# Linear attention in a two-layer transformer stack: value projection reassociated to x^T k, and the output weights folded into one matrix

## Chip, cores, metric

The kernel runs on one core of a Trainium2 chip. The metric is the device time of one execution in microseconds (us), as the median of several runs. Engines: PE is the tensor engine (matmuls), PEld its weight loads, DVE the vector engine, ACT the scalar engine, POOL is GpSimd, SP issues the DMA. The granted clock is the share of its full clock that PE had, by the profile. PE's results land in PSUM, which these kernels use as eight banks; a bank is used again after DVE or ACT has read it out (an eviction).

## The reference, cut to what matters

Four layers in turn, A B A B, on x of 2048 tokens by 1024 features, bf16. A is linear attention with 32 heads of 32; B is a gated feed-forward layer (1024 to 3584 and back), which the change leaves alone.

```python
def A(x, wqkv, wo):                       # x is layer-normed
    q, k, v = split(x @ wqkv)             # 32 heads of 32
    pq, pk = phi(q), phi(k)               # phi(t) = t+1 if t>0 else exp(t), + 1e-6
    kv  = einsum("bhsd,bhse->bhde", pk, v)
    z   = einsum("bhsd->bhd", pk)
    num = einsum("bhqd,bhde->bhqe", pq, kv)
    den = einsum("bhqd,bhd->bhq", pq, z)[..., None] + 1e-6
    return (num / den) @ wo
```

## The kernel before

Tokens come in 16 tiles of 128, four tiles to a group. Each layer A has four projections (k, v, q, out): per projection 16 tiles x 2 halves x 8 matmuls of 128x512. Between them stand the narrow matmuls of the heads, with 132 columns, 128 for four heads' k^T v and four of ones that give z; the same shape again turns q into numerators and denominators.

```python
def kv_unit(t):                           # after k and v of tile t
    for c in range(KD):                   # 8 matmuls, 132 columns each
        nc.tensor.matmul(out=acc[0][:, c, 0:ZW], lhsT=pk[t % 4][:, c * P:(c + 1) * P],
                         rhs=vz[t % 4][:, c, :], ...)
def o_unit(t):                            # numerators and denominators of tile t
    for c in range(KD):                   # 8 matmuls, 132 columns each
        nc.tensor.matmul(out=ps[:, c, 0:ZW], lhsT=pqT[g % 3][:, c, tl * P:(tl + 1) * P],
                         rhs=KVz[:, c, :], start=True, stop=True)
    ...                                   # reciprocal, then one 128x1024 multiply on DVE
def phi(ps, dst):                         # per 128x512 block
    nc.scalar.activation(out=e, in_=ps[:], func=ACT.Exp)
    nc.vector.tensor_scalar(out=e, in0=e, scalar1=1.0, scalar2=1e-6, op0=ALU.min, op1=ALU.add)
    nc.vector.scalar_tensor_tensor(out=dst, in0=ps[:], scalar=1.0 + 1e-6, in1=e, ...)
...
# first layer: per tile two k blocks AND two v blocks, so PE spends 7.4 us on a tile
for t in range(g * TPG, (g + 1) * TPG):
    units += [k_unit(t, 0), k_unit(t, 1)]
    ...
    units += [v_unit(t, 0), v_unit(t, 1)]
```

Normalising a tile takes statistics on DVE, a reciprocal root in small steps on POOL, an apply on DVE, and a transpose: on PE for tiles 0 to 3 of the first layer, by DMA otherwise.

Of the kernel before, what the change touches and what calls it, by code (L numbers as in the profile page):

```python
# [25 lines left out]
def kernel(  # L26
# [23 lines left out]
    MM = 4  # L50
    HC = P // 32
    ZW = P + HC
    ZS = NB // 2
# [13 lines left out]
    KVz = const.tile([P, KD, ZW], BF16, tag="KVz", name="KVz")  # L67

    hT = H[:].rearrange("p (f s) -> p f s", s=G)
    pk = [H[:, i * D:(i + 1) * D] for i in range(4)]  # L70
    o0 = 4 * D
    vz = [H[:, o0 + i * KD * ZW:o0 + (i + 1) * KD * ZW].rearrange("p (c f) -> p c f", f=ZW) for i in range(4)]
    o0 += 4 * KD * ZW
    onat = [H[:, o0 + i * D:o0 + (i + 1) * D] for i in range(4)]
    o0 += 4 * D
    eb = [H[:, o0 + i * NB:o0 + (i + 1) * NB] for i in range(3)]
    oT = [H[:, i * KD * G:(i + 1) * KD * G].rearrange("p (c s) -> p c s", s=G) for i in range(2)]
    wk = Wr[0:2]
    wv = Wr[2:4]
    wo = [Dr[i][:].rearrange("p (k n) -> p k n", n=NB) for i in (0, 1)]  # L80
    pqT = [Dr[i][:].rearrange("p (c s) -> p c s", s=G) for i in (2, 3, 4)]
    wq = [Dr[i][:].rearrange("p (k n) -> p k n", n=NB) for i in (5, 6)]
    wd = [Dr[f // 4][:, (f % 4) * D:(f % 4 + 1) * D] for f in range(KF)]
    ring = [Wr[0], Wr[1], Wr[2], Wr[3], xT[2], xT[3]]

# [12 lines left out]
    def load_k(n):  # L98
        load(wk[n][:], wqkv_v[:, :, D + n * NB:D + (n + 1) * NB])

    def load_v(n):
        load(wv[n][:], wqkv_v[:, :, 2 * D + n * NB:2 * D + (n + 1) * NB])

    def load_q():
        for n in range(2):
            load(wq[n], wqkv_v[:, :, n * NB:(n + 1) * NB])
# [17 lines left out]
    load_x(0)  # L124
    for k in range(0, KD, 2):
        load(wk[0][:, k:k + 2, :], wqkv_v[:, k:k + 2, D:D + NB])
        if k == 0:
            load_x(1)
    load_x(2)
    load_x(3)  # L130
    load_k(1)
    load_v(0)
    load_v(1)
    for t in range(TPG, 2 * TPG):
        load_x(t)
# [6 lines left out]
    mask = const.tile([P, ZW], F32, tag="mask", name="mask")  # L142

    def make_mask():
        nc.gpsimd.memset(mask[:], 0.0)
        for b in range(HC):
            nc.gpsimd.memset(mask[32 * b:32 * b + 32, 32 * b:32 * b + 32], 1.0)
            nc.gpsimd.memset(mask[32 * b:32 * b + 32, P + b:P + b + 1], 1.0)

# [4 lines left out]
    zps = psum.tile([P, NB], F32, tag="mm", bufs=MM, name="zps")  # L154
# [6 lines left out]
    def ln_stats(t):  # L161
        st = small.tile([P, 2, 6], F32, tag="st", name="st")
        for c in range(2):
            nc.vector.bn_stats(out=st[:, c, :], in_=X[:, t, c * NB:(c + 1) * NB])  # L164
        mv = small.tile([P, 2], F32, tag="mv", bufs=2 * TPG, name="mv")
        nc.vector.bn_aggr(out=mv[:], in_=st[:])
        ve = small.tile([P, 1], F32, tag="ve", name="ve")
        nc.gpsimd.tensor_scalar(out=ve[:], in0=mv[:, 1:2], scalar1=1e-5, scalar2=None, op0=ALU.add)
        rstd = small.tile([P, 1], F32, tag="rstd", bufs=2 * TPG, name="rstd")
        nc.gpsimd.tensor_tensor(out=rstd[:], in0=ve[:], in1=mhalf[:], op=ALU.pow)  # L170
        stat[t] = (mv, rstd)

    xns = {}

    def ln_apply(t):
        mv, rstd = stat.pop(t)
        xn = work.tile([P, D], BF16, tag="xn", name="xn")
        nc.vector.tensor_scalar(out=xn[:], in0=X[:, t, :], scalar1=mv[:, 0:1], scalar2=rstd[:],  # L178
                                op0=ALU.subtract, op1=ALU.mult)
        xns[t] = xn  # L180

    def transpose_tile(src, dst):
        nc.sync.dma_start_transpose(out=dst, in_=src)

    def tx(t, slot):

        def run():
            if t not in xns:
                ln_apply(t)
            tl = t % TPG  # L190
            transpose_tile(xns.pop(t)[:], xT[slot][:, :, tl * P:(tl + 1) * P])
        return run

    def tx_pe(t):

        def run():
            if t not in xns:
                ln_apply(t)
            src = xns.pop(t)
            pt = psum.tile([P, KD, P], BF16, tag="mm", bufs=MM, name="pt")  # L200
            for k in range(KD):
                nc.tensor.transpose(out=pt[:, k, :], in_=src[:, k * P:(k + 1) * P], identity=ident[:])
            nc.scalar.copy(out=xT[t // TPG][:, :, t % TPG * P:(t % TPG + 1) * P], in_=pt[:])
        return run

    def mm_tile():
        return psum.tile([P, NB], F32, tag="mm", bufs=MM, name="ps")

    def kv_tile():
        return psum.tile([P, KD, ZS], F32, tag="kv", bufs=1, name="kv")  # L210

    phis = [0]

    def phi(ps, dst):

        e = eb[phis[0] % 3]
        phis[0] += 1
        nc.scalar.activation(out=e, in_=ps[:], func=ACT.Exp)  # L218
        nc.vector.tensor_scalar(out=e, in0=e, scalar1=1.0, scalar2=1e-6, op0=ALU.min, op1=ALU.add)  # L219
        nc.vector.scalar_tensor_tensor(out=dst, in0=ps[:], scalar=1.0 + 1e-6, in1=e, op0=ALU.add, op1=ALU.max)  # L220


    def k_unit(t, n):
        def run():
            ps = mm_tile()
            xt, tl = xT[t // TPG], t % TPG
            for k in range(KD):
                nc.tensor.matmul(out=ps[:], lhsT=xt[:, k, tl * P:(tl + 1) * P], rhs=wk[n][:, k, :],  # L228
                                 start=(k == 0), stop=(k == KD - 1))
            phi(ps, pk[t % 4][:, n * NB:(n + 1) * NB])  # L230
        return run

    def v_unit(t, n):
        def run():
            ps = mm_tile()
            xt, tl = xT[t // TPG], t % TPG
            for k in range(KD):
                nc.tensor.matmul(out=ps[:], lhsT=xt[:, k, tl * P:(tl + 1) * P], rhs=wv[n][:, k, :],  # L238
                                 start=(k == 0), stop=(k == KD - 1))
            c = n * (NB // P)  # L240
            nc.scalar.copy(out=vz[t % 4][:, c:c + NB // P, 0:P], in_=ps[:].rearrange("p (c f) -> p c f", f=P))
        return run

    acc = []

    def kv_unit(t):

        def run():
            if t == 0:
                acc[:] = [kv_tile()]  # L250
            for c in range(KD):
                nc.tensor.matmul(out=acc[0][:, c, 0:ZW], lhsT=pk[t % 4][:, c * P:(c + 1) * P],  # L252
                                 rhs=vz[t % 4][:, c, :], start=(t == 0 and c % 2 == 0),
                                 stop=(t == NT - 1), skip_group_check=True)
            if t == NT - 1:
                nc.vector.tensor_tensor(out=KVz[:], in0=acc[0][:, :, 0:ZW],  # L256
                                        in1=mask[:].unsqueeze(1).to_broadcast([P, KD, ZW]), op=ALU.mult)
        return run

    def q_unit(g, c):  # L260
        def run():
            ps = mm_tile()
            n, cl = c // (NB // P), c % (NB // P)
            for k in range(KD):
                nc.tensor.matmul(out=ps[:], lhsT=wq[n][:, k, cl * P:(cl + 1) * P], rhs=xT[g][:, k, :],  # L265
                                 start=(k == 0), stop=(k == KD - 1))
            phi(ps, pqT[g % 3][:, c, :])
        return run

    def o_unit(t):  # L270

        def run():
            g, tl = t // TPG, t % TPG
            ps = kv_tile()
            for c in range(KD):
                nc.tensor.matmul(out=ps[:, c, 0:ZW], lhsT=pqT[g % 3][:, c, tl * P:(tl + 1) * P],  # L276
                                 rhs=KVz[:, c, :], start=True, stop=True)
            den = small.tile([P, KD, HC], F32, tag="den", name="den")
            nc.vector.tensor_scalar(out=den[:], in0=ps[:, :, P:ZW], scalar1=1e-6, scalar2=None, op0=ALU.add)
            nc.vector.reciprocal(out=den[:], in_=den[:])  # L280
            nc.vector.tensor_tensor(
                out=onat[tl].rearrange("p (c h e) -> p c h e", c=KD, h=HC),
                in0=ps[:, :, 0:P].rearrange("p c (h e) -> p c h e", h=HC),
                in1=den[:].unsqueeze(3).to_broadcast([P, KD, HC, 32]), op=ALU.mult)
        return run

    def to_unit(t):
        def run():
            tl = t % TPG
            transpose_tile(onat[tl], oT[(t // TPG) % 2][:, :, tl * P:(tl + 1) * P])  # L290
        return run
# [5 lines left out]
    def out_unit(t, n):  # L297
        def run():
            ps = mm_tile()
            tl = t % TPG  # L300
            for c in range(KD):
                nc.tensor.matmul(out=ps[:], lhsT=oT[(t // TPG) % 2][:, c, tl * P:(tl + 1) * P], rhs=wo[n][:, c, :],  # L302
# [37 lines left out]
    def stats_unit(t):  # L340
        return lambda: ln_stats(t)

# [178 lines left out]
```

## Time and profile before

| | before |
|---|---|
| time, median of 3 | 1650.54 us (1650.45 to 1650.82) |
| PE busy | 1632.5 of 1648.8 us |
| DVE, ACT busy | 537.9, 250.6 us |
| first layer A (0 to first gate matmul) | 248.64 us |
| first layer B | 580.16 us |
| second layer A | 236.88 us |

From the page of the kernel before: the span, the busy time of each engine with its instructions, and the chain of work that ended last by engine.

```profile
span 1648.8 us, 18785 instructions
...
PE 1632.5 (99%) x7882; PEld 762.9 (46%) x8040; DVE 537.9 (33%) x965; ACT 250.6 (15%) x422; POOL 53.8 (3%) x152
...
PE 98%; DVE 1%; issue 1%; DMA 0%; SPq 0%; POOL 0%; ACT 0%
```

PE is always busy, and the chain is PE from end to end. Every matmul has one weight load, so "PEld x8040" counts the matmuls (a few matmul records are missing, 7882).

The chain in order of time (start, duration, what) gives the cost of one matmul of each size:

```profile
36.11 0.47 PE kv L252 x8
36.58 1.73 PE ps L238 x8
```

Eight matmuls of 132 columns take 0.47 us, eight of 512 take 1.73 us: 59 and 216 ns each. The waits view of PE (who waited for whom, total, times, longest) has three lines:

```profile
PE pt L202 <- DVE xn L178: 2.7, 3, 1.5
PE kv L276 <- DVE KVz L256: 1.4, 2, 0.7
PE zps L156 <- DVE xT_73 L153: 1.2, 1, 1.2
```

### The profile page before, as it was taken

The page shows a single profiled execution, that of the slowest core. Times are in us where ns is not written, and L with a number is a line of the kernel's source. Part 1 is how long each engine was busy: PE and PEld are TensorE (multiplying, and loading weights), DVE is VectorE, ACT ScalarE, POOL GpSimd, SP SyncE. Part 2 cuts the span into 40 slices and gives each one's busy share as a digit, 9 for nine tenths or more (in the row PEclk, how much of TensorE's full clock was granted, in tenths as well). Part 3 has the DMA queues.
Part 4 walks back from the last instruction along what each step waited for, and adds up shares of the span by engine and source line. Part 5 has one row for each costly group of instructions (what it writes and reads, how often), then busy time and mean ns, then how long its engine had stood idle before and what let it go on. Part 6 is the DMA issues. An engine that isn't in the chain of part 4 may idle for free.

```text
span 1648.8 us, 18785 instructions
## 1 busy us (share of the span) xinstructions
PE 1632.5 (99%) x7882; PEld 762.9 (46%) x8040; DVE 537.9 (33%) x965; ACT 250.6 (15%) x422; POOL 53.8 (3%) x152
## 2 busy tenths in 40 slices
PE   9999999999999999999999999999999999999999
PEld 4444544444444444444444445444444444444444
DVE  5553873212211311222443348632132113211211
ACT  3333101100110110011023331011001101100110
POOL 2000000000000000000100000000000000000000
PEclk9999999999999999999999999999999999999999
DMA  6513459431640443063340044594225405422400
GB/s 189 169 26 101 66 115 306 153 103 41 173 155 15 127 154 102 28 177 102 77 128 1 1 115 73 144 306 150 72 68 172 157 23 165 150 81 64 153 4 23
DMA packets 244996, 182.63 MB, mean 111 GB/s; under 512 B 100528, under 2 KB 235696, under 8 KB 244912
## 3 DMA queue, kind: packets, MB, share of 16 engines
q1 hardware_dynamic: 244912, 181.43, 38.5%
q8 instruction: 63, 1.03, 0.3%
q14 instruction: 21, 0.17, 0.0%
HBM read 153.09 MB, written 4.19 MB: 95 GB/s over the span
## 4 chain that ended last, share of the span: by engine, by line
PE 98%; DVE 1%; issue 1%; DMA 0%; SPq 0%; POOL 0%; ACT 0%
PE ps L316 47%; PE ps L333 23%; PE ps L238 7%; PE ps L302 7%; PE ps L265 6%; PE ps L228 6%; PE kv L276 1%; PE kv L252 1%; DMA X<-in_A_x_dram 0%; SPq L96 0%; DVE st L164 0%; DVE KVz L256 0%; DVE D_82 L220 0%; ACT H L218 0%; DVE xn L178 0%
## 5 line engine op out<-in xcount | busy, mean ns | idle before, releaser
L320 DVE TENSOR_TENSOR H<-gs,ps 128x512 bf16<-128x512 f32 x224 | 154.1, 688 | 567.6 <-PE ps L316 530.8
L319 ACT COPY gs<-ps 128x512 f32<-128x512 f32 x224 | 131.3, 586 | 1047.8 <-PE ps L316 1024.9
L333 PEld LDWEIGHTS <-H 128*128 128x128 bf16 x1848 | 178.5, 98 | 208.7
L335 DVE TENSOR_TENSOR X<-X,ps 128x512 bf16<-128x512 bf16 (+1 forms) x66 | 44.2, 670 | 327.0 <-PE ps L333 296.5
L218 ACT ACTIVATE H<-ps 128x512 bf16<-128x512 f32 x128 | 76.4, 597 | 201.8 <-PE ps L228 92.9
L316 PEld LDWEIGHTS <-W_75 128*128 128x128 bf16 x640 | 62.6, 98 | 75.5
L316 PEld LDWEIGHTS <-W_74 128*128 128x128 bf16 x640 | 62.6, 98 | 75.5
L219 DVE TENSOR_SCALAR H<-H 128x512 bf16<-128x512 bf16 x128 | 37.3, 291 | 162.8 <-ACT H L218 162.8
L316 PEld LDWEIGHTS <-xT_73 128*128 128x128 bf16 x576 | 56.4, 98 | 68.0
L316 PEld LDWEIGHTS <-xT_72 128*128 128x128 bf16 x576 | 56.4, 98 | 68.0
L316 PEld LDWEIGHTS <-W_76 128*128 128x128 bf16 x576 | 56.4, 98 | 68.0
L316 PEld LDWEIGHTS <-W_77 128*128 128x128 bf16 x576 | 56.4, 98 | 68.0
L164 DVE BATCH_NORM_STATS2 st<-X 128x6 f32<-128x512 bf16 x128 | 80.8, 673 | 5.4 <-DMA X<-in_A_x_dram 5.4
L316 PE MATMUL ps<-xT_71,W_76 128*128 128x512 bf16 x316 | 75.4, 379 | 0.2
L316 PE MATMUL ps<-xT_70,xT_72 128*128 128x512 bf16 x312 | 75.2, 379 | 0.4
L316 PE MATMUL ps<-xT_70,xT_73 128*128 128x512 bf16 x314 | 75.3, 379 | 0.3
L316 PE MATMUL ps<-xT_71,W_77 128*128 128x512 bf16 x314 | 75.3, 379 | 0.3
L302 PEld LDWEIGHTS <-H 128*128 128x128 bf16 x512 | 49.3, 98 | 56.2
L316 PE MATMUL ps<-xT_71,W_74 128*128 128x512 bf16 x314 | 74.6, 379 | 0.4
L316 PE MATMUL ps<-xT_70,W_74 128*128 128x512 bf16 x314 | 74.6, 379 | 0.3
L316 PE MATMUL ps<-xT_70,W_75 128*128 128x512 bf16 x312 | 74.2, 379 | 0.3
L316 PE MATMUL ps<-xT_71,W_75 128*128 128x512 bf16 x314 | 74.3, 379 | 0.2
(88 smaller groups left out, 1742.9 us busy)
## 6 DMA issues: line engine op xcount, KB each, us to landing
W_74<-in_B_w_gate_dram SPq DMA_DIRECT2D x20, 1024.0 KB, 5.4
W_75<-in_B_w_up_dram SPq DMA_DIRECT2D x20, 1024.0 KB, 7.3
W_76<-in_B_w_gate_dram SPq DMA_DIRECT2D x18, 1024.0 KB, 5.4
W_77<-in_B_w_up_dram SPq DMA_DIRECT2D x18, 1024.0 KB, 7.3
xT_72<-in_B_w_gate_dram SPq DMA_DIRECT2D x18, 1024.0 KB, 5.3
xT_73<-in_B_w_up_dram SPq DMA_DIRECT2D x18, 1024.0 KB, 7.0
X<-in_A_x_dram SPq DMA_DIRECT2D x16, 256.0 KB, 7.8
out_dram<-X SPq DMA_DIRECT2D x31, 128.0 KB, 1.7
```

The costliest lines, as they stand in the source:

```text
L164: nc.vector.bn_stats(out=st[:, c, :], in_=X[:, t, c * NB:(c + 1) * NB])
L218: nc.scalar.activation(out=e, in_=ps[:], func=ACT.Exp)
L219: nc.vector.tensor_scalar(out=e, in0=e, scalar1=1.0, scalar2=1e-6, op0=ALU.min, op1=ALU.add)
L228: nc.tensor.matmul(out=ps[:], lhsT=xt[:, k, tl * P:(tl + 1) * P], rhs=wk[n][:, k, :], start=(k == 0), stop=(k == KD - 1))
L238: nc.tensor.matmul(out=ps[:], lhsT=xt[:, k, tl * P:(tl + 1) * P], rhs=wv[n][:, k, :], start=(k == 0), stop=(k == KD - 1))
L265: nc.tensor.matmul(out=ps[:], lhsT=wq[n][:, k, cl * P:(cl + 1) * P], rhs=xT[g][:, k, :], start=(k == 0), stop=(k == KD - 1))
L302: nc.tensor.matmul(out=ps[:], lhsT=oT[(t // TPG) % 2][:, c, tl * P:(tl + 1) * P], rhs=wo[n][:, c, :], start=(c == 0), stop=(c == KD - 1))
L316: nc.tensor.matmul(out=ps[:], lhsT=w[:, k, j * P:(j + 1) * P], rhs=xT[g % 2][:, k, :], start=(k == 0), stop=(k == KD - 1))
L319: nc.scalar.copy(out=gs[:], in_=gp[:])
L320: nc.vector.tensor_tensor(out=hT[:, f, :], in0=gs[:], in1=up[:], op=ALU.mult)
L333: nc.tensor.matmul(out=ps[:, 0:hi - lo], lhsT=hT[:, f, tl * P:(tl + 1) * P], rhs=wd[f][:, cols], start=(f == 0), stop=(f == KF - 1))
L335: nc.vector.tensor_tensor(out=X[:, t, cols], in0=X[:, t, cols], in1=ps[:, 0:hi - lo], op=ALU.add)
```

## The change

The intent is to take PE work away. k^T v per head needs v = x w_v. It is rewritten as (x^T k) turned by w_v: x^T k is accumulated once over all 16 tiles at full width, then multiplied by w_v per head, masked, and multiplied by the output weights to one 1024x1024 matrix KVo. So the narrow matmuls per tile go. q is divided by the denominators before its transpose, token-major, on DVE; the sums of k for the denominators are running sums on DVE. All x^T k needs all tiles of k, so in the first layer the k stage of 16 tiles stands alone at the start, with no v blocks between. To feed it, part of the normalisation moves to ACT. The eight PSUM banks become one pool.

```diff
+    def xk_unit(j, n):                    # x^T k, 16 matmuls of 512 columns
+            for t in range(NT):
+                nc.tensor.matmul(out=ps[:], lhsT=xn_a[t][:, j * P:(j + 1) * P], rhs=pk[t][:, n * NB:(n + 1) * NB], ...)
+    def over_den(t):                      # the division, token-major
+        nc.vector.tensor_tensor(out=prod, in0=pq[:], in1=zb, op=ALU.mult)
+        nc.vector.tensor_reduce(out=den[:], in_=prod.rearrange("p (h e) -> p h e", e=32), ...)
+        nc.vector.tensor_scalar(out=den[:], in0=den[:], scalar1=1e-6, ...)
+        nc.vector.reciprocal(out=den[:], in_=den[:])
+        nc.vector.tensor_tensor(out=pq[:]..., in0=pq[:]..., in1=den[:]..., op=ALU.mult)
+        tx(pq[:], t, t // TPG)
+    def kvo_unit(c, n):
+        nc.tensor.matmul(out=ps[:], lhsT=KVT[0][:, c, :], rhs=wo[n][:, c, :], start=True, stop=True)
+        if c % 4 == 3:
+            nc.vector.tensor_copy(out=KVo[n][:, c, :], in_=ps[:])
+        else:
+            nc.scalar.copy(out=KVo[n][:, c, :], in_=ps[:])
+    def ln_stats_act(t, xn):              # statistics of one tile in four on ACT
+        nc.scalar.activation(out=xn, in_=X[:, t, :], func=ACT.Identity, accum_out=add[:, 0:1])
+        nc.gpsimd.tensor_scalar(out=mv[:, 1:2], in0=add[:, 0:1], scalar1=-1.0 / D, ...)
+        nc.scalar.activation(out=xn, in_=X[:, t, :], func=ACT.Square, bias=mv[:, 1:2], accum_out=add[:, 1:2])
+        ...                               # variance and reciprocal root on POOL
+    def ln_apply_act(t, xn):              # apply on ACT; its offset on POOL
+        nc.gpsimd.tensor_scalar(out=off[:], in0=mv[:, 0:1], scalar1=rstd[:], scalar2=-1.0, ...)
+        nc.scalar.activation(out=xn, in_=X[:, t, :], func=ACT.Identity, scale=rstd[:], bias=off[:])
 ... first layer, groups 1 to 3 (t is the first tile of the group, u the k blocks of the group before):
+                ln_stats(t)
+                ln_stats_act(t + 1, xn_a[t + 1])
+                u[0]()
+                norm(t)                   # ln_apply_act, then the DMA transpose
+                ln_stats(t + 2)
+                u[1]()
+                norm(t + 1)
 ... then 16 x^T k units, the first 7 (second layer: 4) in a row, the rest between the first 11 q tiles, then
+        kv_unit()
+        do(q[24:28])
+        for i in range(4):
+            kvo_units(i)()
+            q[28 + i]()
```

(Removed lines and buffer changes are left out.)

## The prediction

> **What bounds the kernel now.** TensorE. The page shows PE busy 1632.5 us of 1648.8 (99%), full granted clock in all 40 slices, and the chain that ended last is 98% PE. The waits view of PE lists only 5.3 us. A 128x512 matmul costs 216 ns start to start (eight in 1.73 us in the chain); a 128x132 one of lines 252 and 276 about 59 ns (eight in 0.47 us). DVE is busy 33%, ACT 15%. So time follows the sum of matmul columns, plus about 15 us of ends and start-up stalls.
>
> **What changes on PE.** By the built programs, both layers A together: 512 matmuls of 132 columns go (-30.0 us). Four projections' worth stay: k, q, x^T k in place of v, out. Added are 128 narrow 128x128 (+7.2 us at 56 ns, the spacing of the transposes) and 40 of 512 columns (+8.6 us). Net -14 us, 0.9%, all on the critical path. Layers B, over 70% of the span, stay.
>
> **What changes elsewhere.** The q stage gets heavy on DVE. Per token tile: two phi at 0.98 us (291+692 ns), as before; then the division: product, reduction and scaling over 1024 columns, each estimated at 1.22 us (the trace's 128x1024 fp32 operation takes 1224 ns; the Trainium skill, "VectorE: DVE Perf Modes", perf-mode tier table, gives tensor_reduce and fp32 tensor_tensor only the 1x rate, so no discount), plus 0.18 and 0.35 us. Together 6.2 us per tile. PE has 3.45 us per tile plus interleaved x^T k units: 6.3 us in the first layer, 7.2 in the second, so DVE keeps up for tiles 0 to 10. Tiles 11 to 15 have no such filling: DVE about 5 x 6.2 + 4 = 35 us against 24 of PE. Eight PSUM buffers taken in turn, four KVo evictions queued on DVE behind divisions, let PE run ahead only 4 to 9 us. I estimate 2 to 6 us of stall per layer A, say 4.
>
> Fifteen running sums (1.22 us each) hide behind x^T k units. In the first layer k uses a tile every 3.45 us instead of k and v every 7.4, so normalisation must be faster: DVE 13 us per group of four against 13.8 of PE, helped by ACT (11 us). I give it 0 to 4 us of stalls, say 0.5. Start-up gains about 1 us (first k no longer waits for the second transpose), and the waits for masked KV (1.4 us) go.
>
> **Sum.** 1650.5 - 14 - 2.5 + 8 (q tails) + 0.5 = 1642, 8 in 10 within 1633 to 1652. Within 2%: 0.95; faster 0.02, slower 0.03.
>
> **What would show it.** Right: PE's matmul count and columns fall by 14 us' worth; the waits view of PE shows new waits on DVE (phi, the KVo copy) of 4 to 12 us, at the end of each q stage, DVE over 90% busy there; layers B keep their length to 0.5 us. Each wide division operation takes 1.1 to 1.3 us. The sums stage shows no wait over 2 us.
>
> **What would make it wrong.** Division operations slower than 1.22 us (then tiles 0 to 10 become DVE-bound, up to +1 us per tile per layer for each extra us); DMA transposes of q stuck behind the 4 MB weight loads; layer B starting late, since a gate/up load now waits for the last out unit; no stall at all because the PSUM slack suffices (1632 to 1635).

## More of the kernel before

The timeline of PE shows where the layers begin; the first number is the start in us.

```profile
25.59 1.67 PE L238 MATMUL ps<-W_76,xT_70 128*128 128x512 bf16 x7
...
248.64 1.67 PE L316 MATMUL ps<-xT_70,W_74 128*128 128x512 bf16 x7
...
828.80 1.46 PE L228 MATMUL ps<-W_74,xT_70 128*128 128x512 bf16 x6
...
1065.68 1.67 PE L316 MATMUL ps<-xT_70,W_74 128*128 128x512 bf16 x7
```

The first of these is the first v block: by 25.59 us the eight k blocks of the first group are done. The other three are the start of the first layer B, of the second layer A and of the second layer B; their differences are the stage lengths in the table.

## The result, and the profile after

| | before | changed |
|---|---|---|
| time, median of 4 | 1650.68 us | 1648.53 us (1647.9 to 1649.08) |
| ratio of fast runs | | 0.9986, 95% interval 0.9969 to 1.0004 |
| first layer A | 248.64 us | 251.95 us |
| first layer B | 580.16 us | 580.16 us |
| second layer A | 236.88 us | 231.00 us |

Ratios here are the mean time of one kernel's fast runs over that of the other's fast runs of the same rounds, so they are not quite the ratio of the medians quoted. (The kernel before was timed again here, hence 1650.68.) The forecast was a gain of 8.5 us; the gain was 2.1 us, not told apart from none by its interval. The stage lengths come from single profiles, where they repeat closely: the second layer A took 231.00 or 231.01 us in every run that did not touch it. The start of the program is less steady: the first k block began between 8.35 and 9.09 us in runs whose program is the same up to there, and 9.09 is the profile of the changed kernel itself.

The page of the changed kernel, the same lines as before:

```profile
span 1646.2 us, 18145 instructions
...
PE 1622.5 (99%) x7547; PEld 744.7 (45%) x7696; DVE 646.2 (39%) x1050; ACT 266.8 (16%) x444; POOL 58.0 (4%) x159
...
PE 94%; DVE 3%; issue 1%; ACT 1%; POOL 0%; DMA 0%; ACTq 0%; DVEq 0%
```

The matmuls fell from 8040 to 7696, as counted from the programs. But PE's share of the chain fell from 98% to 94%: DVE, ACT and waits between them now stand on it. The timeline of PE, stage starts:

```profile
251.95 1.24 PE L351 MATMUL ps<-xT_70,W_74 128*128 128x512 bf16 x5
...
832.11 1.24 PE L233 MATMUL ps<-W_74,xT_70 128*128 128x512 bf16 x5
...
1063.11 1.24 PE L351 MATMUL ps<-xT_70,W_74 128*128 128x512 bf16 x5
```

The second layer A became 5.88 us shorter, the first 3.31 us longer; -5.88 + 3.31 is the whole difference of the two spans, 2.6 us. So the question is what the first layer lost. The waits view of PE:

```profile
PE ps L233 <- DMA xT_71<-W_77: 3.9, 1, 3.9
PE ps L233 <- ACT xT_70 L215: 2.2, 2, 1.1
PE ps L233 <- DMA xT_73<-D_84: 2.2, 1, 2.2
PE zps L153 <- DVE xT_73 L150: 1.2, 1, 1.2
PE ps L233 <- DVE pq L225: 1.1, 2, 0.5
PE ps L319 <- DVE D_80 L321: 1.1, 2, 0.5
PE pt L214 <- DVE W_76 L194: 0.6, 1, 0.6
PE ps L233 <- ACT D_81 L323: 0.6, 2, 0.3
```

The two waits for a transposing DMA (3.9 and 2.2 us) are the first tile of group 1 and of group 3 in the first layer's k stage. Waits on DVE and ACT at lines 233 and 319 with two occurrences each are the ends of the two q stages, 1.4 us per layer. The timeline of PE around the first wait:

```profile
24.85 1.89 PE L233 MATMUL ps<-W_75,xT_70 128*128 128x512 bf16 x7
30.68 3.55 PE L233 MATMUL ps<-W_74,xT_71 128*128 128x512 bf16 x8 [3.94 <-DMA xT_71<-W_77]
34.07 1.89 PE L233 MATMUL ps<-W_75,xT_71 128*128 128x512 bf16 x8
```

The last block of group 0 ends at 26.58 (24.85 + 1.73), 1.0 us later than the same eight blocks before the change. Then PE stands for 4.1 us, and the next eight matmuls take 3.39 us instead of 1.73. The stretches view of the changed kernel says why (columns: busy us and instructions of PE, PEld, DVE, ACT, POOL; granted clock; DMA share; GB/s):

```profile
30.60:34.10 3.50, 3.42 (x9) 1.23 (x10) 1.40 (x4) 2.74 (x5) 1.32 (x4) 0.51 0.39 75
```

The granted clock is 0.51. The Trainium skill, "TensorE: Matmul & The Clock Gate", "What's actually happening", states that PE falls back to half clock after an idle window of about 3.4 us and needs a busy one to return. This wait of 4.1 us and the 3.39 us after it agree (the last section has gaps that do not); here the fall costs 1.66 us on top of the wait.

The ledger of the first layer, from these views: late by 1.0 us at the end of group 0, wait 4.1, half clock 1.7, wait for tile 12 2.4 (a matmul's record is 0.16 us longer than its spacing, 379 against 216 ns, so the waits view shows each wait 0.16 us short). That is 9.2 us where the prediction had a net gain of 0.5 (0.5 of stalls less 1 of start). The first term is the least certain: this profile has the latest start of all, by up to 0.7 us.

The chain that led to the first wait, from the timeline of the other engines:

```profile
22.84 0.57 POOL L169 TENSOR_TENSOR rstd<-ve,mhalf 128x1 f32<-128x1 f32 x1
23.49 0.25 POOL L182 TENSOR_SCALAR mv<-add 128x1 f32<-128x1 f32 x1
...
23.77 1.15 ACT L183 ACTIVATE W_77<-X,mv 128x1024 bf16<-128x1024 bf16 x1 [1.85 <-POOL mv L182]
...
24.92 0.58 ACT L223 ACTIVATE e<-ps 128x512 bf16<-128x512 f32 x1
...
25.53 0.29 DVE L224 TENSOR_SCALAR e<-e 128x512 bf16<-128x512 bf16 x1 [3.09 <-ACT e L223]
...
25.93 0.27 POOL L201 TENSOR_SCALAR off<-mv,rstd 128x1 f32<-128x1 f32 x1
26.23 1.24 ACT L203 ACTIVATE W_77<-X,off,rstd 128x1024 bf16<-128x1024 bf16 x1 [0.73 <-POOL off L201]
```

Tile 4's reciprocal root is ready at 23.41 us, but its offset, a tiny operation, runs on POOL only at 25.93: in program order the variance and root of tile 5, which wait for its second moment on ACT, stand in front of it. The Trainium skill, "Perfetto Trace Analysis", "Tensor Engine Instruction (MATMUL, LD_WEIGHTS)", calls the queues of ACT, DVE and GPSIMD strictly first in, first out; these lines agree. Meanwhile ACT had waited 1.85 us for POOL, whose turn had come late because tile 4's statistics stood ahead there; and DVE waited 3.09 us for ACT's exp. No engine is full, all wait for each other. From the end of the apply at 27.47 to PE's next matmul at 30.68 another 3.2 us go to the transpose by DMA, so the 2.5 us of queueing are most of the 4.1 us wait and not all of it.

### The profile page after: what moved, and what is told of

Its sections match the earlier page's. It is cut to its first block, busy times and chain, and to the rows that moved or that the text cites. A ratio compares the mean times of both kernels' runs of the same rounds, so it can differ in the third digit from the quotient of the medians.

```text
span 1646.2 us, 18145 instructions
## 1 busy us (share of the span) xinstructions
PE 1622.5 (99%) x7547; PEld 744.7 (45%) x7696; DVE 646.2 (39%) x1050; ACT 266.8 (16%) x444; POOL 58.0 (4%) x159
## 4 chain that ended last, share of the span: by engine, by line
PE 94%; DVE 3%; issue 1%; ACT 1%; POOL 0%; DMA 0%; ACTq 0%; DVEq 0%
PE ps L351 47%; PE ps L368 23%; PE ps L233 10%; PE ps L337 7%; PE ps L245 7%; DVE st L161 1%; DVE H L225 1%; ACT e L223 0%; PE zps L153 0%; DVE pq L225 0%; DVE e L224 0%; DVE D_82 L289 0%; DVE den L291 0%; POOL rstd L169 0%; ACT D_81 L323 0%
## 5 line engine op out<-in xcount | busy, mean ns | idle before, releaser
L368 PEld LDWEIGHTS <-H 128*128 128x128 bf16 x1848 | 178.6, 98 | 208.7
L223 ACT ACTIVATE e<-ps 128x512 bf16<-128x512 f32 x128 | 75.8, 595 | 174.7 <-PE ps L233 163.4
L161 DVE BATCH_NORM_STATS2 st<-X 128x6 f32<-128x512 bf16 x122 | 77.4, 675 | 2.3 <-DMA X<-in_A_x_dram 2.3
L368 PE MATMUL ps<-D_81,H 128*128 128x512 bf16 (+2 forms) x264 | 66.0, 373 | 0.4
L368 PE MATMUL ps<-D_78,H 128*128 128x512 bf16 (+2 forms) x262 | 65.9, 372 | 0.3
```

Of the source, the lines that this page charges most:

```text
L161: nc.vector.bn_stats(out=stat[t][0][:, c, :], in_=X[:, t, c * NB:(c + 1) * NB])
L223: nc.scalar.activation(out=e[:], in_=ps[:], func=ACT.Exp)
L368: nc.tensor.matmul(out=ps[:, 0:hi - lo], lhsT=hT[:, f, tl * P:(tl + 1) * P], rhs=wd[f][:, cols], start=(f == 0), stop=(f == KF - 1))
```

## The experiments

Theory A: the first layer's k stage ate the gain, by waits on normalisation. Rivals: B, the waits only show a limit of DVE and ACT in that stage; C, the division at the end of the q stages costs more than it shows. Changes are against the changed kernel unless said otherwise. It was timed once, before the experiments; only the kernel before was timed in the same rounds as each of them. Differences between medians of about 1 us therefore say little, and the stage lengths decide: the k stage (last column) took 67.05 to 67.10 us in all five profiles in which nothing of it was touched.

| run | time, us | first layer A | second layer A | first k to first x^T k |
|---|---|---|---|---|
| changed | 1648.53 | 251.95 | 231.00 | 67.10 |
| k reads group 0 (wrong result) | 1646.52 | 250.37 | 231.00 | 66.03 |
| order only | 1647.05 | 251.38 | 231.00 | 66.60 |
| no tail division (wrong result) | 1643.14 | 249.17 | 228.91 | 67.07 |
| filler matmuls | 1648.27 | 251.57 | 231.01 | 67.26 |
| banks in turn (1 run, unknown) | 1657.76 | 257.24 | 235.48 | 68.78 |
| new start | 1641.87 | 245.84 | 231.01 | 60.59 |
| product on GpSimd | 1656.06 | 255.12 | 234.95 | 67.06 |
| combined | 1641.51 | 248.31 | 228.91 | 60.84 |
| KVo on ACT (1 run, unknown) | 1643.15 | 249.21 | 228.90 | 67.07 |
| KVo on ACT, timed | 1643.64 | 249.56 | 228.90 | 67.05 |
| even pace | 1634.74 | 241.09 | 228.90 | 57.98 |

The kernel before, beside these, had medians of 1650.43 to 1650.64 us. The last column is the k stage of the first layer; its 256 matmuls need 55.3 us at 216 ns.

### k reads group 0

```diff
-        xt, tl = xT[t // TPG], t % TPG
+        xt, tl = xT[0], t % TPG          # k of the first layer only; wrong result on purpose
```

> Wrong result on purpose: in the first layer the k units of groups 1 to 3 read the transposed tiles of group 0, so that they wait for no normalisation; nothing else changes. Theory A (the first layer's k stage ate the gain: PE stood 3.9 us for tile 4 and 2.2 us for tile 12, and ran 1.7 us long at half clock after the first wait): the two waits and the slow matmuls go, the time falls by 7.8 us, from 1648.5 to about 1640.7. Rival B (those waits hide a limit of DVE and ACT throughput in that stage): the waits move to PSUM buffers and the gain is under 3 us. Rival C (the loss is the division at the end of the q stages): under 1 us.

The time fell by 2.0 us, not 7.8, and the profile has 0.5 us of it as an earlier start and 1.1 us in the k stage. The waits on the DMA were gone, but the waits view of PE in this run begins with a line that was not there:

```profile
PE ps L233 <- DVE H L225: 6.0, 7, 1.3
```

PE ran ahead until the PSUM banks were full and then waited for DVE's phi. So theory A in its simple form fell, and rival B was nearer: whatever PE is spared at one place, the stage makes it wait at another. In this run DVE was busy 36.7 and ACT 35.9 of the 55 us from 20 to 75 us, so the limit was not the throughput of either; DVE spent 16.9 us of that stretch waiting for ACT's exp, as it does in the changed kernel.

### Order only

```diff
-                ln_stats(t)
-                ln_stats_act(t + 1, xn_a[t + 1])
-                u[0]()
-                norm(t)
+                stats_act_1(t + 1, xn_a[t + 1])   # first moment; its two POOL steps
+                ln_stats(t)
+                stats_act_2(t + 1, xn_a[t + 1])   # second moment on ACT
+                norm(t)                           # offset and apply of tile t
+                stats_act_3(t + 1)                # POOL: variance, root of tile t+1
+                u[0]()
```

> Correct result; the same instructions, but in the first layer GpSimd and ScalarE no longer see tile t+1's second moment in front of tile t's offset and apply. Theory A1 (the wait for tile 4 is in-order queueing: its rstd was ready at 23.4 us and its apply began at 26.2 us): apply of tile 4 begins near 23.8 us, the first wait shrinks from 3.9 to about 1.5 us, the half-clock stretch after it goes[...], the wait for tile 12 goes; a gain of 4 to 7 us, about 1643. Rival A2 (latency of the transposing DMA or late arrival of x): first wait over 3 us still, gain under 2 us.

The gain of 4 to 7 us did not come. The same instructions in another order shortened the k stage by 0.5 us; the medians lie 1.5 us apart, the profiles 0.6. The first wait shrank from 3.9 to 1.5 us and full clock held, as expected; but tile 5, whose statistics on ACT came later now, brought a new wait of 1.9, and group 3 had two, of 1.6 and 2.0 us. The queueing is real, and moving it costs elsewhere.

### No tail division

```diff
+        if t >= 11:                       # wrong result on purpose
+            tx(pq[:], t, t // TPG)
+            return
         nc.vector.tensor_tensor(out=prod, in0=pq[:], in1=zb, op=ALU.mult)
```

> Wrong result on purpose: token tiles 11 to 15 skip the division by the denominators in both layers. By the waits view (1.4 us of PE waits at the end of each q stage) 2.8 us go, 1645.7. My prediction (4 us each): 8 us, 1640.5. Rival C (division is the main loss): 6 us or more.

The second layer A fell from 231.00 to 228.91 us, the first by 2.78, of which 0.64 was an earlier start. So the end of a q stage costs 2.1 us, 4.2 in both layers: half of the predicted 4 per layer. The waits view shows 1.4 of it, in three waits that are each 0.16 us short.

### Filler matmuls

```diff
+                if g == 2:
+                    idle = mm_tile()
+                    for _ in range(16):
+                        nc.tensor.matmul(out=idle[:], lhsT=ones[:], rhs=xT[0][:, 0, :], start=True, stop=True)
```

> Correct result; 16 matmuls that nobody reads (3.45 us) stand in the 3.9 us in which PE waits for tile 4. If the eight matmuls after that wait took 3.39 instead of 1.73 us because the clock had dropped during the wait, they are back at 1.73 us and the time falls by about 1.7 us, to 1646.9. If they were slow for another reason (a PSUM buffer, an operand not there), no change, 0 to +0.5 us.

The cause of the slow matmuls is confirmed: with PE kept busy through the wait, the clock in the same stretch (the columns as before) stays at 1.00 and 17 matmuls fit where 9 had.

```profile
30.30:33.80 3.50, 3.47 (x17) 1.59 (x18) 1.46 (x4) 2.74 (x4) 1.26 (x4) 1.00 0.39 75
```

But the time was the same (1648.27, expected 1646.9). The 1.7 us came back as a longer wait for tile 12, whose transpose landed when it did before:

```profile
62.00 13.99 PE L233 MATMUL ps<-W,xT 128*128 128x512 bf16 x62 [3.46 <-DMA xT<-D]
```

It had been 2.23 us with the next matmul at 62.37. This says again that the normalisation of later tiles sets the pace of the stage.

### Banks in turn

```diff
-        return psum.tile([P, NB], F32, tag="mm", bufs=8, name="ps")
+        return psum.tile([P, NB], F32, tag=turn(), bufs=1, name="ps")   # mm0 .. mm7, strictly in turn
```

> Correct result; the changed kernel with its eight PSUM buffers taken strictly in turn, as my prediction assumed; in the built changed kernel the pool hands them out in another order (at the end of the q stage the projection of tile 14's second half gets the buffer that tile 13's first half left, eleven allocations earlier). If the order of buffers is why the waits at the end of each q stage were 1.4 us and not the 4 to 6 us of my hand count, they now come to 4 to 6 us per layer, and the time rises by 5 to 9 us. If not, they stay near 1.4 us per layer.

This tests a step of the prediction. The second layer A grew from 231.00 to 235.48 us, so the end of a q stage cost 6.6 us (2.1 + 4.5). The waits view of PE, both layers together:

```profile
PE ps L325 <- DVE D L327: 4.9, 2, 2.4
PE ps L325 <- DVE pq L231: 4.2, 6, 1.2
```

That is 4.5 us of waits per layer, near the predicted 4; part of the rest is a lower clock after them (0.50 from 195 to 197 us). It is one run, but both layers show the same waits.

In the built changed kernel the pool does not hand out banks in turn (tile 14's second half takes the bank of eleven allocations earlier), and its order had saved two thirds of that cost. By what rule it picks was not looked into.

### New start

```diff
             ln_apply(1, xn_a[1])
-            k[0]()
             tx_pe(xn_a[1], 1)
             bn(2, 1)
             moments(2)
             ln_apply(2, xn_a[2])
+            k[0]()
+            ln_stats(3)
 ...
+            ln_stats(4)                   # before k of tile 2
 ...
-                ln_stats(t)               # groups 2 and 3 (group 1 alike)
-                ln_stats_act(t + 1, xn_a[t + 1])
-                u[0]()
-                norm(t)
+                u[0]()
+                ln_stats(t)
+                for i in range(1, TPG):
+                    u[i]()
+                    norm(t + i - 1)
+                    ln_stats(t + i)       # all statistics on DVE, one unit ahead of their apply
```

> Correct result; the first layer's k stage is re-ordered: statistics all on VectorE and one unit ahead of their apply, no statistics on ScalarE, tile 4's statistics before k of tile 2, the second transpose before the first k. Theory A' (after the first four runs: VectorE waits for ScalarE's exp, which queues behind applies that wait for GpSimd, and PE then waits for either; none of the engines is full, DVE 68% and ACT 65% busy in the stage): the k stage ends 6 to 10 us earlier, time 1639 to 1642. Rival B' (VectorE throughput: two phi per unit pair and all statistics come to 13.9 us per group against 13.8 of PE): waits for PSUM buffers remain, gain under 3 us.

The k stage took 60.59 us instead of 67.10, and the time fell by 6.7 us. DVE did more work than in the changed kernel (all statistics: 38.4 us busy from 20 to 70 us against 31.9), and the stage became shorter, so DVE's throughput was not the limit. But this run is not a change of order alone: the same edit took the statistics off ACT (28.5 us busy there against 32.8, neither near 50), and how much each part gave was not separated. One wait of 2.2 us for tile 4 remained, again with an offset on POOL (21.79 us) behind another tile's root (tile 4's own was ready at 19.37), and half clock after it.

### Product on GpSimd

```diff
-        nc.vector.tensor_tensor(out=prod, in0=pq[:], in1=zb, op=ALU.mult)
+        (nc.gpsimd if t >= 11 else nc.vector).tensor_tensor(out=prod, in0=pq[:], in1=zb, op=ALU.mult)
```

> Correct result; for token tiles 11 to 15 GpSimd multiplies q by the sums instead of VectorE (1.22 us each). If the end of the q stage is bound by VectorE's work, as the run without the division there showed (2.1 us per layer A), most of it goes: gain 2 to 4 us, 1644.5 to 1646.5. If GpSimd takes over 3 us for a 128x1024 product, tile by tile it becomes the bound and the time stays or rises by up to 3 us.

Worse by 7.5 us; the expected gain of 2 to 4 did not come. The product took 2139 ns on GpSimd against 1225 on DVE, and DVE, in order, waited for it: 11.6 us in the first layer, 23.2 in both. The Trainium skill, "GPSIMD Engine Reference", "Engine selection", gives about twice the time of VectorE for operations with two inputs; here it is 1.75 times. Work that the next step of the same chain needs at once is not taken off an in-order engine by sending it away.

### Combined

The new start, with tile 4's apply before tile 5's statistics, all KVo evictions on ACT, and x^T k units spread over 12 q tiles.

```diff
+            norm(4)
             ln_stats(5)
             k[3]()
-            norm(4)
 ...
-        if c % 4 == 3:
-            nc.vector.tensor_copy(out=KVo[n][:, c, :], in_=ps[:])
-        else:
-            nc.scalar.copy(out=KVo[n][:, c, :], in_=ps[:])
+        nc.scalar.copy(out=KVo[n][:, c, :], in_=ps[:])
 ...
-        for t in range(11):               # q tiles with x^T k units between them
+        for t in range(12):
```

> Correct result; the new start of the run before, plus: tile 4's apply stands before tile 5's statistics (in that run its rstd was ready at 19.4 us, but GpSimd computed its offset at 21.8 us, behind tile 5's rstd, and PE waited 2.2 us); all KVo evictions on ScalarE; the x^T k units spread over 12 q tiles instead of 11. Theory A' (in-order coupling at the start) expects the 2.2 us wait and the slow matmuls after it to go, about 3 us. The reading of the q tail (bound by VectorE's work, 2.1 us per layer) expects another 2 to 4 us from the two layers. Together 1641.9 - 5 to 7 = 1635 to 1637. If the tail is bound by the single chain of division steps and not by work, only the first 3 us come: 1639.

A miss: 1641.51 where 1635 to 1637 was expected, no better than the new start. The wait for tile 4 went and the second layer A lost its 2.1 us, but the first layer gave both back: tile 12 now came 2.3 us late, and the output weights, loaded after the last x^T k unit, 2.4 us late, each followed by half clock.

### KVo evictions on ACT

This tells the parts of the run before apart: the same edit of the KVo evictions on the changed kernel, nothing else.

> Correct result; the changed kernel with the four KVo evictions per pass of VectorE moved to ScalarE, nothing else, to tell this part of the run before from the spreading. The prediction named these evictions, queued behind divisions, as part of the tail. If so: the waits of the KVo matmuls for VectorE (1.1 us in all) go and each layer A shortens by 0.5 to 1.5 us. If PE waits for ScalarE instead, no change.

> The same kernel as in the look with all KVo evictions on ScalarE, now timed in rounds. Its profile had each layer A 2.1 us shorter, as with no division at all in the tail. Expected: 4 to 5 us under the changed kernel's 1648.5, so 1643.5 to 1644.5.

The second layer A took 228.90 us, the same as with no division at all, and PE has no wait left at the end of the q stage. These 2.1 us are more than the 0.5 to 1.5 expected. The time was 1643.64, 4.9 us under the changed kernel (in the two profiles 0.2 and 0.6 us of it are an earlier start). The stretches view of the changed kernel and of this one, over 26 us at the end of the first q stage:

```profile
171.00:197.00 26.00, 24.43 (x158) 12.77 (x159) 24.78 (x40) 11.39 (x23) 0.00 (x0) 1.00 0.97 268
```

```profile
168.00:194.00 26.00, 25.89 (x168) 13.74 (x169) 24.80 (x38) 13.63 (x26) 0.00 (x0) 1.00 0.88 251
```

DVE is as full as before, 24.8 of 26 us, and PE no longer cares. What had stopped PE was not that DVE was full, but banks that PE needed soon and that were not yet emptied. The edit changed two things there, though. Building both programs again shows that the pool also hands out other banks from tile 14's second half on: that projection gets the bank of a KVo copy of six allocations earlier, where the changed kernel gave it the one of eleven earlier, which DVE's phi still held (its 0.55 us wait). Of the changed kernel's three waits there, one was for a phi on DVE, one for a KVo copy on DVE and one for a KVo copy on ACT. How much came from the engine and how much from the banks was not separated.

### Even pace

The combined kernel with 11 q tiles again, and one tile's statistics after every second k block instead of four after the first four.

```diff
-                u[0]()
-                ln_stats(t)
-                for i in range(1, TPG):
-                    u[i]()
-                    norm(t + i - 1)
-                    ln_stats(t + i)
+                for i in range(TPG):
+                    u[2 * i]()
+                    if i or g > 2:
+                        norm(t + i - 1)
+                    ln_stats(t + i)
+                    u[2 * i + 1]()
```

> Correct result; the combined kernel with two repairs: the x^T k units over 11 q tiles again (with 12 the output weights came 2.4 us late in the first layer), and in the first layer one tile's statistics after every second k unit instead of four after the first four (tile 12's statistics began at 47.6 us there, behind a backlog of phi on VectorE, and PE waited 2.3 us, followed by slow matmuls). If the backlog is local, the first k stage now runs without a wait after its start: 4 to 6 us less than the combined kernel's 1641.5, 1635.5 to 1637.5. If VectorE's throughput binds (38.4 us busy of 50 in that stage so far), waits of 2 us or more remain somewhere in it and the gain is under 3 us.

1634.74 us, a little below the expected 1635.5 to 1637.5; ratio 0.9904 to the kernel before (95% interval 0.9889 to 0.9919): about 1% faster, clear of noise, with the correct result. All waits of PE in this run:

```profile
PE pt L214 <- DVE W L194: 1.3, 1, 1.3
PE zps L153 <- DVE xT L150: 1.2, 1, 1.2
PE ps L233 <- DMA xT<-XW: 0.8, 2, 0.5
PE ps L233 <- DMA xT<-W: 0.5, 1, 0.5
```

Against the kernel before, the first layer A is 7.55 us shorter and the second 7.98. The stretch from 20 to 70 us in the changed kernel and in this one (columns as before):

```profile
20.00:70.00 50.00, 43.62 (x192) 19.21 (x194) 31.87 (x69) 32.78 (x46) 14.12 (x42) 0.97 0.47 98
```

```profile
20.00:70.00 50.00, 48.69 (x225) 21.56 (x223) 41.45 (x90) 29.00 (x40) 11.85 (x34) 1.00 0.62 141
```

DVE is busy 41.5 of the 50 us, more than in any other version of the stage: it was not DVE's throughput. From the combined kernel to this one the k stage went from 60.84 to 57.98 us by the order of the same work, so here 2.9 us are order alone.

## Why the prediction was right or wrong

- **PE work, -14 us: right.** With the waits gone the second layer A is 7.98 us shorter, 7.1 of matmuls and about 0.9 for the wait of the numerators for the masked KV (L276 on L256 before, 0.7 in the waits view) that went. The matmul count is the one foretold.
- **Layers B unchanged: right.** The first took 580.16 us both times.
- **The division's cost: right.** The groups view of the changed kernel (busy us, mean ns):

```profile
L289 DVE TENSOR_TENSOR D_82<-pq,D_83 128x1024 f32<-128x1024 bf16 x32 | 39.2, 1225 | 1.1
L295 DVE TENSOR_TENSOR pq<-pq,den 128x1024 bf16<-128x1024 bf16 x32 | 39.2, 1225 | 1.1
L291 DVE TENSOR_REDUCE den<-D_82 128x32 f32<-128x1024 f32 x32 | 39.0, 1220 | 1.1
```

  The estimate was 1.22 us: the 1224 ns of an operation of this width in the trace before, without a discount, since the Trainium skill's "VectorE: DVE Perf Modes", perf-mode tier table, gives tensor_reduce and fp32 tensor_tensor the 1x rate alone; the trace agrees. The sums stage showed no wait.
- **The q tails, +8 us: right mechanism, wrong size.** They cost 4.2 us (run without the division there). The step that failed is "eight PSUM buffers taken in turn": taken in turn, the waits come to 4.5 us per layer, near the predicted 4 (6.6 us with all that follows). The built program assigns banks otherwise, and could have been read before. With the KVo evictions, which the prediction named as one part, on ACT nothing of the 2.1 us is left; that edit also changed the banks.
- **The first layer's start and k stage, +0.5 - 1 us: wrong, and the reason for the miss.** It cost about 9 us. The failed step is "DVE 13 us per group of four against 13.8 of PE, helped by ACT (11 us)": it compared throughputs of engines and took the difference for slack. But a tile goes DVE, POOL, ACT, DMA before PE can use it, all queues run in program order, and the order interleaved tiles so that each queue held up the next. With the order mended and the statistics moved from ACT to DVE (more DVE work), the stage fell from 67.1 to 58.0 us. The half clock after a wait, 1.7 us, was not thought of at all. By luck the errors partly cancelled: 9.7 us too little here, 3.8 too much at the q tails.

The sum with measured terms: -14 - 1.4 (KV mask waits) + 4.2 + 9.2 = -2.0 us; the medians differ by 2.1, the two profiles by 2.6.

What stays open: how the 9 us split between single orderings, and between order and the work that left ACT. The runs show that the stage is paced by coupled queues and not by DVE's throughput, and that two orders of the same work cost different amounts (60.84 and 57.98 us), not which one line is to blame.

## What to carry to other kernels

Where a change takes filling work out of a stage, don't check the engines by their busy time per unit alone: follow one unit through the queues in program order, small operations on side engines included, because a 0.3 us step can stand 2.5 us behind another unit's. If removing one wait of PE makes another appear, stop removing waits and look for what paces the stage. Put evictions that the bottleneck engine will need soon on an engine whose queue has no long jobs ahead of them, and read the bank assignment from the built program instead of assuming rotation.

## What the Trainium skill lacked or had wrong

- "TensorE: Matmul & The Clock Gate" ("What's actually happening", "HAM oscillation") puts the fall to half clock at idle gaps over about 3.4 us. Here gaps with 2.25, 2.30 and 2.41 us in the waits (new start, combined kernel twice) were followed by some 3.4 us at a granted clock of 0.54 to 0.56, while one of 3.46 us (filler matmuls, tile 12) and one of 2.23 us (changed kernel, tile 12) were followed by 1.00. A free-running window, as the page describes it, could let the 3.46 us pass; but a window of 3.4 us that is idle throughout does not fit into gaps of under 2.6 us (waits plus the 0.16 us). The 3.4 us of these two sections are no safe line in either direction.
- "Perfetto Trace Analysis" says that a matmul's end in the profile is a model. It does not say what this does to waits: with a record of 379 ns and a spacing of 216 ns, each wait of PE is shown about 0.16 us short (3.94 shown, 4.1 from the end by spacing to the next start).
- "GPSIMD Engine Reference" is right in its factor (1.75 measured, about 2 stated); no page that was read warns that the apply of a normalisation can wait behind another tile's small POOL steps, 2.5 us here.
- Nothing that was read treats the order in which a PSUM pool hands out banks; in this kernel it was worth 4.5 us in the second layer A (one run).
